# Pooled attention with a gated mixing layer on one core: attention's steps at other places in the emission order, the tail queries' last 128 scores beside the last maximum, and the weights' scratch tile in three padded blocks

## The chip, the core and the metric

The kernel runs on one core of one Trainium2 chip. The metric is device time in microseconds (us), the median of several executions; less is better. The engines are named as the profile names them: PE multiplies (PEld is its weight load), DVE is VectorE, ACT is ScalarE, POOL is GpSimd, SP issues the DMAs.

## The reference

All inputs are float32; q, k and v are 8 batches x 8 heads x 1152 x 64. What is computed, cut to its core:

```python
q_pool = q.reshape(B, H, S // 2, 2, D).mean(axis=3)          # 576 queries a head
scores = scale * np.matmul(q_pool, k.transpose(0, 1, 3, 2))  # 576 x 1152
scores = scores - np.max(scores, axis=-1, keepdims=True)
attn = np.exp(scores)
attn = attn / (np.sum(attn, axis=-1, keepdims=True) + 1e-09)
x = heads_side_by_side(np.matmul(attn, v))                   # 8 x 576 x 512
theta = x @ w_theta
y = w_tok_r @ (x * cos(theta)) + w_tok_i @ (x * sin(theta))  # over tokens
u = x + y
out = u + np.maximum(u @ w_ch, 0.0)
```

## The kernel before

The first part does attention, two heads at a time: 32 pairs `i`, in 18 score steps each (`u` is one of two halves of 288 pooled queries, `kt` one of nine blocks of 128 keys). The second part does the mixing layer; the change does not touch it.

For a pair, `prep_t` transposes keys and pooled queries on PE (`pt`, group 0 and group 1), ACT rounds them into `hi`, DVE takes the rest into `lo`. `maxpass` makes the row maxima: 12 steps of two matmuls (`pm`) and one DVE reduction each (L332). The last 64 queries of both heads share one tile, `tail`; `max_tail` multiplies it with keys 0 to 1023 (`px`) and, on L348, with the last 128 keys, whose result goes into the unused end of the next pair's `pt` tile; L351 and L352 reduce them. `max_nm` negates the maxima, `max_row` turns them (`pmt`) and copies them (`mT`), and `load_max` puts them as rows into `nmr` by four DMAs. `escore` is one score step: eight matmuls into one tile `pe` (hi x hi, hi x lo, lo x hi, and the maxima's row), then one exponential on ACT into `pc` (L393, 14 buffers). `av` is a run of matmuls of the nine `pc` of a half with `vn` (36 rows in the trace) into `pa`. `ssum` adds the `pc` up on POOL, `norm_sum` sums over the partitions (`pns`), and a chain of small DMAs with a reciprocal (L451) brings the divisors back for `norm_out` (L473).

All PSUM tiles of this part have two banks and go through four slots. `bank2` gives a new tile the slot that its own bookkeeping (the costs `HOLD`, three running clocks) holds to be free first. A tile's first matmul waits until the slot's last tile has been read.

The order on every engine is the order of emission. `plan` gives each step of each pair a position (18 positions to a pair, a score step at each whole one) and sorts them all. `burst` puts several steps at one position: with u = 0 it is transposes of group 1 for pair i+2, the maxima's row of pair i+1, `av` and the sums of pair i-1; with u = 1 it is `tail_prep` (transposes of group 0 for pair i+3 and `max_tail` of pair i+2) and `av`.

Beside all this, `weights` narrows the mixing layer's float64 weights to float32 in 18 jobs, one step at each position of `W_AT`. In `narrow` five DVE instructions with one input and one with two (L556) run on 128x512 or 128x576 words between the tiles `raw`, `wf` and `ws`.

Of the kernel before, what the change touches and what calls it, by code (L numbers as in the profile page):

```python
# [9 lines left out]
F32 = mybir.dt.float32  # L10
# [14 lines left out]
W_AT = (9.45, 9.5, 9.85, 10.5, 12.75, 18.0, 18.6, 19.25, 20.45)  # L25
# [4 lines left out]
MAX_AT1 = (-18.1, -16.8, -16.1, -15.35, -14.7, -14.0, -13.3, -12.6, -11.7, -10.3, -9.8, -9.0)  # L30
PLAN = {
    "load_q": -44.55,
    "load_k": -43.62,
    "pool_q": -35.35,
    "load_max": -7.6,
    "load_v": -7.0,
    "max_nm": -8.85,
    "norm_spread": 29.0,
    "norm_load": 29.15,
    "norm_recip": 37.5,  # L40
    "norm_save": 37.6,
    "norm_bcast": 37.7,
    "norm_out": 46.5,
    "norm_store": 46.6,
}
MAN = ("PE", "Activation", "DVE", "Pool", "SP")
BANKS = {}
SLOTS = 4
HOLD = {
    "e": (0.54, "a", 0.6),  # L50
    "pm": (0.17, "d", 0.95),
    "pt": (0.75, "ad", 2.1),
    "px": (0.6, "d", 1.55),
    "pa": (4.4, "a", 0.4),
    "mt": (0.2, "a", 0.3),
    "ns": (1.0, "a", 0.5),
    "pw": (0.75, "ad", 1.9),
}
BANKS2 = {"h": 1, "t": 1, "m": 4, "r": 2}
# [30 lines left out]
OT_LAG = 1.0  # L90
CH_BANK = "mrmr"
TINY = 2.0**-15
MAGIC = 12582912.0
# [8 lines left out]
def pooled_attention_moe_kernel(  # L102
# [58 lines left out]
    def bank2(kind, name):  # L161
        n = min(range(SLOTS), key=lambda k: slots[k])
        work, engines, after = HOLD[kind]
        clock["p"] = max(clock["p"], slots[n]) + work
# [43 lines left out]
    with ExitStack() as p1:  # L208
# [128 lines left out]
        def max_tail(i, pt):  # L337
# [7 lines left out]
            st["pm", 0] = pm  # L345
            if pt is None:
                pt = bank2("px", f"py{i}")
# [55 lines left out]

        def av(i, u):
            st = state[i]
            if u == 0:
                st["xu"] = nrm.tile([P, 2, HALF], F32, tag="xu", name=f"xu{i}", bufs=3)
            pa = bank2("pa", f"pa{i}_{u}")
            for kt in range(KT):
# [8 lines left out]
            nc.scalar.copy(st["xu"][:, u, :], pa[:, 0, 0:HALF])  # L418

        def norm_sum(i, px):  # L420
# [14 lines left out]
            sm = st["sm"] = sml.tile([P, HALF], F32, tag="sm", name=f"sm{i}", bufs=1)  # L435
            nc.scalar.activation(sm, px[:, 1, 0:HALF], AF.Identity, bias=eps)

        def norm_spread(i):
# [35 lines left out]

        def burst(i, u):
            if u == 0:
                if i + 2 < NPAIR:
                    prep_all(i + 2, 1)
                if i + 1 < NPAIR:
                    max_row(i + 1)  # L480
                av(i, u)
                if i > 0:
                    norm_sum(i - 1, bank2("ns", f"pns{i}"))
            else:
                tail_prep(i)
                av(i, u)

        def prep_all(i, g):
# [7 lines left out]

        def tail_prep(i):
            more = i + 3 < NPAIR
            if more:
                prep(i + 3)  # L500
                prep_t(i + 3, 0)
            if i + 2 < NPAIR:
                max_tail(i + 2, state[i + 3]["pt", 0] if more else None)
            if more:
                prep_hi(i + 3, 0)
                prep_lo(i + 3, 0)

# [8 lines left out]
        def weights():  # L516
# [7 lines left out]

            def fetch(parts, n):
                ws = wst.tile([P, SQ], F32, tag="ws", name="ws")
                raw = wst.tile(
                    [P, SQ, 2 if wide else 1], U32 if wide else F32, tag="raw", name="raw"
                )
                for dst, src in parts:  # L530
                    nc.sync.dma_start(raw[dst, 0:n], src)
                return raw, ws

            def narrow(raw, ws, R, n, g):
                dst = ws[0:R, 0:n].rearrange("a (t p) -> a p t", t=g)
                if not wide:
                    nc.vector.tensor_copy(
                        dst, raw[0:R, 0:n, 0].rearrange("a (p t) -> a p t", t=g)
                    )
# [7 lines left out]
                nc.scalar.activation(tl, lo, AF.Copy, scale=2.0**-44)  # L547
                nc.vector.tensor_scalar(f, hi, 0x7FFFFFFF, None, ALU.bitwise_and)
# [14 lines left out]
                yield  # L563
                nc.gpsimd.tensor_tensor(
                    dst,
                    f.bitcast(F32).rearrange("a (p t) -> a p t", t=g),
                    tl.rearrange("a (p t) -> a p t", t=g),
                    ALU.add,
                )
                yield  # L570
# [7 lines left out]
            def square(wv, c, dst):  # L578
                yield
                raw, ws = fetch([(slice(0, P), wv[:, c])], DM)  # L580
                yield
# [86 lines left out]
        def plan(i):  # L668
# [7 lines left out]
            if i < 2:  # L676
                at(PRO[i][1], 3, prep_all, i, 1)
                at(PRO[i][2], 3, max_tail, i, None)
            if i == 0:
                at(-7.8, 3, max_row, i)  # L680
            at(base + pl["load_max"], 7, load_max, i)
            at(base + pl["load_v"], 5, load_v, i)
# [8 lines left out]
            for u in range(2):  # L691
                at(base + AV_AT[u], 4, burst, i, u)
            for n, fn in (
# [10 lines left out]
        for i in range(NPAIR):  # L704
            plan(i)
        at(NU * NPAIR + 2, 9, lambda: norm_sum(NPAIR - 1, bank2("ns", "pend")))
        pw = ExitStack()
# [303 lines left out]
```

## Time and profile before

| | us |
|---|---|
| median of 3 runs (1397.08 to 1399.8) | 1399.42 |
| the profiled execution | 1395.23 |
| its span, first to last instruction | 1393.2 |
| first and last `pmt`, one in each of 32 pairs | 25.2 and 856.0 |

| engine | busy us | share of the span |
|---|---|---|
| PE | 1342.4 | 96% |
| POOL | 914.4 | 66% |
| DVE | 864.6 | 62% |
| ACT | 724.0 | 52% |

A busy PE is not a PE at its peak: a matmul that waits for its weights counts as busy. So for PE the starts of successive instructions say more than the busy share.

### The profile page before, as it was taken

The numbers are of one execution on the slowest core, as the hardware profiler recorded it, in microseconds if no ns is written. First come the engines' busy times: TensorE is split into PE (matmuls) and PEld (weight loads), VectorE is DVE, ScalarE is ACT, GpSimd is POOL, SyncE is SP. The second block draws the span as 40 slices with busy tenths as digits, with TensorE's granted clock in tenths as the row PEclk, the third lists the DMA queues.
The fourth block names the chain that finished last, engine by engine and source line by source line (L and its number), as shares of the span: only waits on it lengthen the run. The fifth ranks groups of instructions, "written<-read, shape, count | busy, mean of one in ns | idle before, by whom it ended". The sixth has DMA issues, their size and how long they took to land.

```text
span 1393.2 us, 29952 instructions
## 1 busy us (share of the span) xinstructions
PE 1342.4 (96%) x12178; PEld 1088.3 (78%) x12178; DVE 864.6 (62%) x1143; ACT 724.0 (52%) x1250; POOL 914.4 (66%) x672
## 2 busy tenths in 40 slices
PE   5999999999999999999999999899999999999998
PEld 3777777776777677777777777698999999999998
DVE  5867776776667776777677765465363453535442
ACT  1556565565556555565555565365454444445341
POOL 1789888989898998889898898742332322233220
PEclk9999999999999999999999999999999999999999
DMA  4334343334433444333443333221111211111111
GB/s 102 101 87 117 89 110 103 110 100 117 110 85 96 114 115 106 93 111 85 128 112 87 82 83 99 74 78 39 35 46 35 62 42 35 39 35 46 27 35 35
DMA packets 130906, 111.66 MB, mean 80 GB/s; under 512 B 95040, under 2 KB 95424, under 8 KB 130768
## 3 DMA queue, kind: packets, MB, share of 16 engines
q1 hardware_dynamic: 130592, 109.28, 28.9%
q8 instruction: 96, 1.57, 0.5%
q0 software_dynamic: 176, 0.46, 0.1%
q14 instruction: 42, 0.34, 0.1%
HBM read 88.29 MB, written 21.27 MB: 79 GB/s over the span
## 4 chain that ended last, share of the span: by engine, by line
PE 72%; DVE 15%; ACT 7%; DMA 3%; issue 2%; POOL 1%; SPq 0%; ACTq 0%; POOLq 0%; DVEq 0%
PE pe L390 18%; PE pa L411 17%; PE py L841 11%; PE pth L763 7%; PE pr L880 6%; DVE mx L332 5%; PE pt L285 4%; PE pm L325 3%; PE pns L427 2%; ACT pc L393 2%; PE pxn L751 1%; DVE r L785 1%; DVE r L786 1%; PE po L903 1%; DVE mx L351 1%
## 5 line engine op out<-in xcount | busy, mean ns | idle before, releaser
L402 POOL TENSOR_TENSOR ss<-ss,pc 128x576 f32<-128x576 f32 x384 | 561.8, 1463 | 68.9 <-ACT pc L393 45.8
L332 DVE TENSOR_REDUCE mx<-pm 128x2 f32<-128x768 f32 x384 | 347.5, 951 | 125.6 <-PE pm L325 124.0
L393 ACT ACTIVATE pc<-pe 128x576 f32<-128x576 f32 x576 | 364.8, 652 | 98.2 <-PE pe L390 85.6
L411 PE MATMUL pa<-pc,vn 128*64 128x288 f32 x2304 | 293.5, 409 | 0.9 <-PE pmt L362 0.8
L814 POOL TENSOR_TENSOR Z<-ab,Z 128x512 fp32r<-128x512 f32 x40 | 51.6, 1291 | 309.4 <-ACT Z L810 274.1
L411 PEld LDWEIGHTS pa<-pc,vn 128*64 128x64 f32 x2304 | 162.2, 137 | 109.4 <-issue 5.4
L841 PE MATMUL py<-wtk,Z 128*128 128x288 f32 x1728 | 242.0, 297 | 0.0
L841 PEld LDWEIGHTS py<-wtk,Z 128*128 128x128 f32 x1728 | 233.2, 189 | 1.5 <-ACT Z L810 0.2
L390 PE MATMUL pe<-hi 64*128 64x288 f32 x1152 | 202.7, 345 | 12.3 <-DVE mx L332 7.3
L390 PEld LDWEIGHTS pe<-hi 64*128 64x128 f32 x1152 | 109.5, 184 | 83.2 <-ACT pc L393 34.0
L390 PE MATMUL pe<-nmr,oner 64*128 64x288 f32 x1152 | 171.9, 291 | 2.2 <-DMA nmr<-mT 2.2
L390 PE MATMUL pe<-lo,hi 64*128 64x288 f32 x1152 | 172.2, 293 | 0.0
L390 PE MATMUL pe<-hi,lo 64*128 64x288 f32 x1152 | 172.0, 292 | 0.0
L325 PE MATMUL pm<-hi 64*128 64x384 f32 x768 | 137.5, 354 | 9.1 <-DVE mx L332 4.7
L390 PEld LDWEIGHTS pe<-nmr,oner 64*128 64x128 f32 x1152 | 110.5, 185 | 2.6 <-DMA nmr<-mT 2.6
L390 PEld LDWEIGHTS pe<-lo,hi 64*128 64x128 f32 x1152 | 111.0, 186 | 0.0
L390 PEld LDWEIGHTS pe<-hi,lo 64*128 64x128 f32 x1152 | 110.4, 185 | 0.0
L312 DVE TENSOR_TENSOR lo<-pt,hi 128x768 fp32r<-128x768 f32 x64 | 67.6, 1056 | 64.5 <-ACT hi L301 64.5
L880 PEld LDWEIGHTS pr<-us,wch 128*128 128x128 f32 x768 | 104.5, 188 | 2.0
L880 PE MATMUL pr<-us,wch 128*128 128x288 f32 x768 | 105.8, 295 | 0.0
L301 ACT CAST hi<-pt 128x768 fp32r<-128x768 f32 x64 | 56.2, 878 | 84.4 <-DVE mx L352 68.1
L402 POOL TENSOR_TENSOR ss<-pc,pc 128x576 f32<-128x576 f32 x64 | 93.8, 1466 | 5.9 <-ACT pc L393 5.9
(105 smaller groups left out, 1657.9 us busy)
## 6 DMA issues: line engine op xcount, KB each, us to landing
qn<-in_q_dram SPq DMA_DIRECT2D x32, 576.0 KB
kn<-in_k_dram SPq DMA_DIRECT2D x64, 288.0 KB
vn<-in_v_dram SPq DMA_DIRECT2D x32, 576.0 KB
dn<-ro SPq DMA_DIRECT2D x64, 144.0 KB
xd<-xu SPq DMA_DIRECT2D x32, 288.0 KB
xT<-xd SPq DMA_DIRECT2D x8, 1152.0 KB
out_dram<-on SPq DMA_DIRECT2D x23, 192.0 KB
out_dram<-on SPq DMA_DIRECT2D x23, 128.0 KB
```

What stands on the lines that cost most here:

```text
L285: nc.tensor.transpose(out=pt[:, n, c : c + R], in_=src.rearrange("p h d -> p (h d)"), identity=ident[0:R, 0:R],)
L301: nc.scalar.copy(hi, src)
L312: nc.vector.tensor_tensor(lo, src, hi.bitcast(F32), ALU.subtract)
L325: nc.tensor.matmul(pm[:, h, 0:W], hi[hs, Q0 + j * P : Q0 + (j + 1) * P], hi[hs, K0[3 * g] : K0[3 * g] + W], start=True, stop=True,)
L332: nc.vector.tensor_reduce(mx[:, j : j + 5 : 4, g : g + 1], pm[:, :, 0:W], AX.X, ALU.max)
L390: nc.tensor.matmul(pe[:, h, 0:HALF], w[hs], x[hs], start=(n == 0), stop=(n == 3))
L393: nc.scalar.activation(pcs[u, kt], pe[:, :, 0:HALF], AF.Exp, scale=SC)
L402: nc.gpsimd.tensor_tensor(st["ss", u], first, st["pc"][u, kt], ALU.add)
L411: nc.tensor.matmul(pa[hs, 0, 0:HALF], st["vn"][:, h, kt, :], st["pc"][u, kt][:, h, :], start=(kt == 0), stop=(kt == KT - 1),)
L763: nc.tensor.matmul(th, xs[c][:, j * P : (j + 1) * P], ws[:, c], start=(n == 0), stop=(n == 11))
L841: nc.tensor.matmul(st["py", c, u][:, 0:HALF], Z[zi][:, c * P : (c + 1) * P], wtk[wi][:, kw, u * HALF : (u + 1) * HALF], start=(i == 0 and ...
L880: nc.tensor.matmul(pr[u][:, 0:HALF], wch[wi][:, c, e * P : (e + 1) * P], st["us", ui][:, c, u * HALF : (u + 1) * HALF], start=(n == 0), st ...
```

## The change

- All steps get positions of their own in place of `burst` and `tail_prep`: the transposes, their `hi` and `lo`, the tail copy, `max_tail` and the maxima's row by the table `PREP_AT`, the sums by `NS_AT`. All other positions and the costs in `HOLD` have new numbers. `av` can now be split into pieces, but the table asks for nine steps in one piece.
- The tail's product with the last 128 keys goes into free columns of the last `pm` tile of `maxpass`, with its reduction right behind that tile's. The separate tile `py` that some pairs used is gone.
- In `narrow` the scratch tile `wf` has three blocks of a third of the columns, 194 words apart. The one-input instructions now have one side in three blocks and the other side plain; 512 columns become 513, with one more small DMA for the last one in 8 of the 18 jobs. The first shift writes `wf` instead of `raw`.

```diff
-MAX_AT = (-24.9, -23.65, -22.55, -20.85, -19.55, -18.8, -15.55, -14.35, -13.5, -11.6, -10.2, -9.15)
-SS_LAG = 4.5
-AV_AT = (10.35, 19.25)
+MAX_AT = (-25.08, -24.951, -24.126, -21.989, -17.714, -16.703, -16.481, -16.035, -13.864, -10.761, -9.027, -7.903)
+SS_LAG = 5.493
+AV_AT = (((10.593, 9),), ((19.957, 9),))
+PREP_AT = {'t0': -34.901, 'hi0': -34.757, 'px': -9.4, 'lo0': -34.733, 't1': -26.381, 'hi1': -26.225, 'lo1': -25.86, 'tail': -25.662, 'row': -7.096}
+NS_AT = 29.431
...
+WF_COLS = 194
...
+                    rest = j == 3 and g == 2
+                    if rest:
+                        nc.tensor.matmul(
+                            pm[:, 0, W:], st["tail"], hi[:, K0[8] : K0[8] + P], start=True, stop=True
+                        )
                     nc.vector.tensor_reduce(
                         mx[:, j : j + 5 : 4, g : g + 1], pm[:, :, 0:W], AX.X, ALU.max
                     )
+                    if rest:
+                        nc.vector.tensor_reduce(mx[:, 8, 2:3], pm[:, 0, W:], AX.X, ALU.max)
...
-            nc.tensor.matmul(
-                pt[:, 0, 3 * P :], tl, hi[:, K0[8] : K0[8] + P], start=True, stop=True
-            )
             nc.vector.tensor_reduce(mx[:, 8, 0:2], pm, AX.X, ALU.max)
-            nc.vector.tensor_reduce(mx[:, 8, 2:3], pt[:, 0, 3 * P :], AX.X, ALU.max)
...
-                lo, hi = raw[0:R, 0:n, 0], raw[0:R, 0:n, 1]
-                f = wst.tile([P, SQ], U32, tag="wf", name="wf")[0:R, 0:n]
+                n = 3 * -(-n // 3)
+                f = wst.tile([P, 3, WF_COLS], U32, tag="wf", name="wf")[0:R, :, 0 : n // 3]
...
+                lo, hi = three(raw[0:R, 0:n, 0]), three(raw[0:R, 0:n, 1])
                 tl = lo.bitcast(F32)
-                mk = ws[0:R, 0:n]
-                nc.vector.tensor_scalar(lo, lo, 8, None, ALU.logical_shift_right)
+                mk = three(ws[0:R, 0:n])
+                nc.vector.tensor_scalar(f, lo, 8, None, ALU.logical_shift_right)
```

Three places show what moves. The names carry no pair number: in what follows the `pe` rows are pair 14's, `pm` and `px` are pair 15's unless it says otherwise. First, PE just behind `av` of the half u = 1. Before:

```order
L390 MATMUL pe_02_5782<-hi_4941 128x288 x2
L390 MATMUL pe_02_5782<-lo_4942,hi_4941 128x288 x2
L390 MATMUL pe_02_5782<-hi_4941,lo_4942 128x288 x2
L390 MATMUL pe_02_5782<-nmr_108,oner 128x288 x2
L325 MATMUL pm_20_5792<-hi_5341 128x384 x2
L390 MATMUL pe_03_5800<-hi_4941 128x288 x2
L390 MATMUL pe_03_5800<-lo_4942,hi_4941 128x288 x2
L390 MATMUL pe_03_5800<-hi_4941,lo_4942 128x288 x2
L390 MATMUL pe_03_5800<-nmr_108,oner 128x288 x2
L325 MATMUL pm_21_5810<-hi_5341 128x384 x2
```

The same place after:

```order
L372 MATMUL pe_02_5781<-hi_4939 128x288 x2
L372 MATMUL pe_02_5781<-lo_4940,hi_4939 128x288 x2
L372 MATMUL pe_02_5781<-hi_4939,lo_4940 128x288 x2
L372 MATMUL pe_02_5781<-nmr_108,oner 128x288 x2
L372 MATMUL pe_03_5793<-hi_4939 128x288 x2
L372 MATMUL pe_03_5793<-lo_4940,hi_4939 128x288 x2
L372 MATMUL pe_03_5793<-hi_4939,lo_4940 128x288 x2
L372 MATMUL pe_03_5793<-nmr_108,oner 128x288 x2
L372 MATMUL pe_04_5807<-hi_4939 128x288 x2
L372 MATMUL pe_04_5807<-lo_4940,hi_4939 128x288 x2
L372 MATMUL pe_04_5807<-hi_4939,lo_4940 128x288 x2
L372 MATMUL pe_04_5807<-nmr_108,oner 128x288 x2
```

Before, score and maximum steps take turns; after, three score steps stand in a row and then one maximum step (`pm_22`) follows.

Second, PE around `av` of the half u = 0 (`pmt` is pair 15's row of maxima, `pt_16` pair 16's transposes of group 1). Before:

```order
L390 MATMUL pe_11_5911<-nmr_108,oner 128x288 x2
L285 MATMUL pt_16_5921<-ident,qp_5722 128x96 x6
L285 MATMUL pt_16_5921<-ident,kn_5573 128x128 x3
L362 MATMUL pmt_5935<-ident,nm_5901 9x128
L411 MATMUL pa_0_5940<-pc_00_5707,vn_5594 64x288 x2
```

After (here `pm_00` and `pm_01` are pair 16's and `pns` the sums of pair 13):

```order
L398 MATMUL pa_0_5939<-pc_08_5864,vn_5713 64x288 x2
L344 MATMUL pmt_5960<-ident,nm_5932 9x128
L307 MATMUL pm_00_5965<-hi_5731 128x384 x2
L372 MATMUL pe_12_5970<-hi_4939 128x288 x2
L372 MATMUL pe_12_5970<-lo_4940,hi_4939 128x288 x2
L372 MATMUL pe_12_5970<-hi_4939,lo_4940 128x288 x2
L372 MATMUL pe_12_5970<-nmr_108,oner 128x288 x2
L307 MATMUL pm_01_5980<-hi_5731 128x384 x2
L419 MATMUL pns_5984<-ss_13_5450,ones 32x288
```

The row of maxima moved from ahead of the nine `av` steps to right behind them; the sums, which stood directly behind `av`, now stand behind a score step and two maximum steps; the transposes of group 1 moved up by a score and a maximum step.

Third, DVE over the same time (`lo` is pair 16's). Before:

```order
L332 TENSOR_REDUCE mx_5598<-pm_30_5853 128x2
L332 TENSOR_REDUCE mx_5598<-pm_31_5870 128x2
L332 TENSOR_REDUCE mx_5598<-pm_32_5886 128x2
L357 TENSOR_REDUCE nm_5901<-mx_5598 128x9
L548 TENSOR_SCALAR wf<-raw 128x512
L550 TENSOR_SCALAR ws<-wf 128x512
L552 TENSOR_SCALAR wf<-ws 128x512
L312 TENSOR_TENSOR lo_5737<-pt_16_5921,hi_5736 128x960
```

After:

```order
L319 TENSOR_REDUCE mx_5565<-pm_30_5859 128x2
L334 TENSOR_REDUCE mx_5565<-px_5876 128x2
L319 TENSOR_REDUCE mx_5565<-pm_31_5881 128x2
L530 TENSOR_SCALAR wf<-raw 128x3x171
L532 TENSOR_SCALAR ws<-wf 128x513
L319 TENSOR_REDUCE mx_5565<-pm_32_5925 128x2
L323 TENSOR_REDUCE mx_5565<-pm_32_5925 128x1
L294 TENSOR_TENSOR lo_5732<-pt_16_5903,hi_5731 128x960
L339 TENSOR_REDUCE nm_5932<-mx_5565 128x9
```

The reduction of `px` moved here from the other half of the pair, and the negated maxima `nm` now stand behind two weight instructions and `lo`.

## Rows read from the trace of the kernel before

**Rows 1.** Busy time over pairs 1 to 29 of attention, by engine.

```profile
core 0: us, PE busy (x) PEld busy (x) DVE busy (x) ACT busy (x) POOL busy (x), PEclk, DMA share, GB/s
58.50:842.50 784.00, 766.14 (x8053) 565.50 (x8051) 569.46 (x672) 457.54 (x798) 698.98 (x507) 1.00 0.38 101
```

**Rows 2.** Tile `pmt`, once a pair: ns min/median/max, first and last start.

```profile
L362 PE MATMUL pmt<-ident,nm x32: 269/273/372, 25.2 to 856.0; 128*9 128x128 f32 x32
```

**Rows 3.** Timeline of PE, 400 to 430 us: start, us, engine, line, idle before.

```profile
401.40 0.69 PE L427 MATMUL pns<-ss,ones 128*32 128x288 f32 x8
...
402.51 0.40 PE L390 MATMUL pe<-hi 64*128 64x288 f32 x2
...
410.59 0.29 PE L390 MATMUL pe<-nmr,oner 64*128 64x288 f32 x2
410.81 0.87 PE L285 MATMUL pt<-ident,kn 128*128 128x128 f32 x6
...
412.14 4.59 PE L411 MATMUL pa<-pc,vn 128*64 128x288 f32 x36
416.65 0.40 PE L390 MATMUL pe<-hi 64*128 64x288 f32 x2
...
417.29 0.34 PE L325 MATMUL pm<-hi 64*128 64x384 f32 x2
417.46 0.29 PE L390 MATMUL pe<-hi 64*128 64x288 f32 x2
...
417.99 0.34 PE L325 MATMUL pm<-hi 64*128 64x384 f32 x2
418.20 0.40 PE L390 MATMUL pe<-hi 64*128 64x288 f32 x2
...
424.52 0.71 PE L285 MATMUL pt<-ident,qp 96*128 96x96 f32 x6
...
425.61 4.59 PE L411 MATMUL pa<-pc,vn 128*64 128x288 f32 x36
```

**Rows 4.** Timeline of the other engines, and PE, in the same stretch.

```profile
417.49 1.35 ACT L393 ACTIVATE pc<-pe 128x576 f32<-128x576 f32 x2 [0.32 <-PE pe L390]
...
418.54 1.45 DVE L545 TENSOR_SCALAR raw<-raw 128x512 uint32<-128x512 uint32 x1
...
420.91 0.40 PE L390 MATMUL pe<-hi 64*128 64x288 f32 x2 [1.22 <-DVE mx L332]
```

**Rows 5.** Groups by shape: busy us, mean ns, idle us before, releasers.

```profile
L332 DVE TENSOR_REDUCE mx<-pm 128x2 f32<-128x768 f32 x384 | 347.5, 951 | 125.6 <-PE pm L325 124.0
L390 PE MATMUL pe<-hi 64*128 64x288 f32 x1152 | 202.7, 345 | 12.3 <-DVE mx L332 7.3 <-DVE wtk L184 0.8 <-ACT tail L308 0.8
L390 PE MATMUL pe<-lo,hi 64*128 64x288 f32 x1152 | 172.2, 293 | 0.0
L351 DVE TENSOR_REDUCE mx<-px 128x2 f32<-128x1024 f32 x32 | 39.0, 1219 | 18.9 <-PE px L342 18.7
L312 DVE TENSOR_TENSOR lo<-pt,hi 128x960 fp32r<-128x960 f32 x32 | 37.0, 1155 | 32.2 <-ACT hi L301 32.2
L451 DVE RECIPROCAL rc<-rc 128x9 f32<-128x9 f32 x32 | 6.5, 204 | 1.2 <-DMA rc<-rd 1.2
L610 PE MATMUL pwt<-ident,ws 128*128 128x128 f32 x32 | 5.2, 286 | 0.0
```

**Rows 6.** Who waited for whom, PE's weight loads: us, times, longest.

```profile
PEld pe L390 <- ACT pc L393: 34.0, 134, 0.7
PEld pe L390 <- issue: 23.2, 55, 0.5
```

**Rows 7.** Single lines: ns min/median/max, first and last start.

```profile
L552 DVE TENSOR_SCALAR wf<-ws x18: 444/1375/2096, 61.0 to 839.7; 128x512 uint32<-128x512 uint32 x8, 128x576 uint32<-128x576 uint32 x8, 64x576 uint32<-64x576 uint32 x2
L556 DVE SCALAR_TENSOR_TENSOR wf<-raw,wf x18: 677/1480/2393, 66.1 to 843.8; 128x512 uint32<-128x512 uint32 x8, 128x576 uint32<-128x576 uint32 x8, 64x576 uint32<-64x576 uint32 x2
L370 SPq DMA_DIRECT2D nmr<-mT x64: 612/636/1033, 30.5 to 858.0; - x64
```

More of the change, by code (lines that the diff above doesn't have):

```diff
@@ L163, in bank2 @@
         work, engines, after = HOLD[kind]
+        psum["slot"] = n
         clock["p"] = max(clock["p"], slots[n]) + work
@@ L402, in ssum, with av @@
             nc.gpsimd.tensor_tensor(st["ss", u], first, st["pc"][u, kt], ALU.add)
-        def av(i, u):
+        def av(i, u, first, n):
             st = state[i]
[L406 to L409, printed above, removed]
+            if first == 0:
+                if u == 0:
+                    st["xu"] = nrm.tile([P, 2, HALF], F32, tag="xu", name=f"xu{i}", bufs=3)
+                st["pa", u] = bank2("pa", f"pa{i}_{u}")
+                st["slot"] = psum["slot"]
+                if n < KT:
+                    slots[st["slot"]] = 1e9
+            pa = st["pa", u]
+            for kt in range(first, first + n):
                 for h, hs in enumerate(HEADS):
@@ L417, in av @@
                     )
-            nc.scalar.copy(st["xu"][:, u, :], pa[:, 0, 0:HALF])
+            if first > 0:
+                clock["p"] += AV_WORK * n
+            if first > 0 and first + n == KT:
+                slots[st["slot"]] = clock["p"] + 0.8
+            if first + n == KT:
+                nc.scalar.copy(st["xu"][:, u, :], pa[:, 0, 0:HALF])
         def norm_sum(i, px):
@@ L436, in norm_sum, with norm_sums @@
             nc.scalar.activation(sm, px[:, 1, 0:HALF], AF.Identity, bias=eps)
+        def norm_sums(i):
+            norm_sum(i, bank2("ns", f"pns{i}"))
         def norm_spread(i):
@@ L495, in prep_all, with prep_first @@
                 prep_tail(i)
[L497 to L506, printed above, removed]
+        def prep_first(i):
+            prep(i)
+            prep_t(i, 0)
         def norm_store(i):
@@ L523, in words, with fetch @@
                 return w.bitcast(U32).rearrange("r (e o) -> r e o", o=2)
-            def fetch(parts, n):
+            def fetch(parts, n, more=None):
                 ws = wst.tile([P, SQ], F32, tag="ws", name="ws")
@@ L531, in fetch, with three @@
                     nc.sync.dma_start(raw[dst, 0:n], src)
+                if wide and more is not None:
+                    nc.sync.dma_start(raw[:, n : n + 1], more)
                 return raw, ws
             def narrow(raw, ws, R, n, g):
-                dst = ws[0:R, 0:n].rearrange("a (t p) -> a p t", t=g)
                 if not wide:
                     nc.vector.tensor_copy(
-                        dst, raw[0:R, 0:n, 0].rearrange("a (p t) -> a p t", t=g)
+                        ws[0:R, 0:n].rearrange("a (t p) -> a p t", t=g),
+                        raw[0:R, 0:n, 0].rearrange("a (p t) -> a p t", t=g),
                     )
                     return
-                lo, hi = raw[0:R, 0:n, 0], raw[0:R, 0:n, 1]
-                f = wst.tile([P, SQ], U32, tag="wf", name="wf")[0:R, 0:n]
+                n = 3 * -(-n // 3)
+                f = wst.tile([P, 3, WF_COLS], U32, tag="wf", name="wf")[0:R, :, 0 : n // 3]
+                def three(x):
+                    return x.rearrange("a (b c) -> a b c", b=3)
+                lo, hi = three(raw[0:R, 0:n, 0]), three(raw[0:R, 0:n, 1])
                 tl = lo.bitcast(F32)
-                mk = ws[0:R, 0:n]
-                nc.vector.tensor_scalar(lo, lo, 8, None, ALU.logical_shift_right)
+                mk = three(ws[0:R, 0:n])
+                nc.vector.tensor_scalar(f, lo, 8, None, ALU.logical_shift_right)
                 yield
-                nc.scalar.activation(tl, lo, AF.Copy, scale=2.0**-44)
+                nc.scalar.activation(tl, f, AF.Copy, scale=2.0**-44)
                 nc.vector.tensor_scalar(f, hi, 0x7FFFFFFF, None, ALU.bitwise_and)
@@ L563, in narrow @@
                 yield
[L564 to L569, printed above, removed]
+                if g == 1:
+                    dst, a, b = mk, f.bitcast(F32), tl
+                else:
+                    dst = ws[0:R, 0:n].rearrange("a (t b r) -> a b r t", t=g, b=3)
+                    a = f.bitcast(F32).rearrange("a b (r t) -> a b r t", t=g)
+                    b = tl.rearrange("a b (r t) -> a b r t", t=g)
+                nc.gpsimd.tensor_tensor(dst, a, b, ALU.add)
                 yield
@@ L677, in plan @@
                 at(PRO[i][1], 3, prep_all, i, 1)
-                at(PRO[i][2], 3, max_tail, i, None)
+                at(PRO[i][2], 3, max_tail, i)
             if i == 0:
                 at(-7.8, 3, max_row, i)
+            for n, (name, fn, args) in enumerate((
+                ("t0", prep_first, (i,)), ("hi0", prep_hi, (i, 0)), ("lo0", prep_lo, (i, 0)),
+                ("t1", prep_t, (i, 1)), ("hi1", prep_hi, (i, 1)), ("lo1", prep_lo, (i, 1)),
+                ("tail", prep_tail, (i,)), ("px", max_tail, (i,)), ("row", max_row, (i,)),
+            )):
+                if i >= (3, 3, 3, 2, 2, 2, 2, 2, 1)[n]:
+                    at(base + PREP_AT[name], 3, fn, *args)
             at(base + pl["load_max"], 7, load_max, i)
@@ L691, in plan @@
             for u in range(2):
-                at(base + AV_AT[u], 4, burst, i, u)
+                first = 0
+                for pos, n in AV_AT[u]:
+                    at(base + pos, 4, av, i, u, first, n)
+                    first += n
+            at(base + NS_AT if i < NPAIR - 1 else NU * NPAIR + 2, 9, norm_sums, i)
             for n, fn in (
```

52 lines of the change are left out of this document (7 added, 45 removed).

## Prediction

> **What bounds the kernel now.** I read the busy time of the attention stage first. Over 784 us of it PE is busy for 766.14 at a granted clock of 1.00; POOL comes next with 698.98, then DVE with 569.46 [rows 1]. So PE sets the pace, and POOL leaves room to shorten a pair only from 26.8 to about 23.9 us. The maxima's row is transposed once in each of 32 pairs, from 25.2 to 856.0 us [rows 2]: (856.0 - 25.2) / 31 = 26.80 us a pair.
>
> Then I read PE's timeline for what a pair would take if nothing waited [rows 3]. A score step is 0.53 (417.46 to 417.99), a maximum step 0.17 (417.29 to 417.46), a run of `av` 4.51 (412.14 to 416.65), transposes of group 0 with the tail's products 1.33 (410.81 to 412.14), group 1 with the maxima's row 1.09 (424.52 to 425.61), the sums 1.11 (401.40 to 402.51). That makes 18 x 0.53 + 12 x 0.17 + 2 x 4.51 + 1.33 + 1.09 + 1.11 = 24.13. Two more things belong to it. The last two matmuls before a transposition take 0.22 in place of 0.13 (410.59 to 410.81), twice a pair; the first score step behind `av` or the sums takes 0.64 (416.65 to 417.29), 0.11 more than the others, again twice. So 24.53, and 0.17 for the weights' transposes (5.2 us over 31 pairs [rows 5]): 24.70. The other 2.10 us of a pair are waits.
>
> These waits have two sources. The first is slot reuse. The score step at 416.65 ends at 417.29; its exponential starts at 417.49 and takes 0.68 (1.35 for two), so its slot is free at 418.17 [rows 3, 4]. Only 0.87 us of PE work (a maximum, a score, a maximum) lies between, and the step at 418.20 that takes the slot shows 0.40 in place of 0.29: its weights could not be loaded ahead. Over the run the first matmuls of score steps take 345 ns against 293 for the others [rows 5], and PE's loads waited 134 times for an exponential, 34.0 us in all [rows 6]. The second is DVE: a weight instruction of 1.45 us at 418.54 puts the maxima behind it, and PE stands 1.22 us at 420.91 [rows 4].
>
> **The change part by part.** *Slots and turn-taking.* With the new numbers the slots rotate over three other tiles, in most places 1.22 us of PE work (two scores and a maximum). The exponential needs 0.20 + 0.68 = 0.88, so 0.34 is to spare. What eats it is ACT itself: three scores in a row take PE 1.59, their exponentials 2.04, so each adds 0.15 of backlog. Walking through the new order with these durations, I find one late slot between `av` of u = 1 and `av` of u = 0, and two in the other half: 3 x 0.11 = 0.33 us a pair. Maximum steps, which took turns with scores (one in 0.70 us of PE, 0.95 of DVE [rows 5]), are now spread over the pair, so I charge no more for them. What is late next is ACT, by about 0.1 us at several places.
>
> *Weight instructions.* The five with one input took 444 ns at best and 1375 in the median for L552; that spread shows a wait for something outside DVE, and POOL is busy nine tenths of that time [rows 1, 7]. In three blocks I take 0.68, the best of L556 with two inputs, which gets no faster form [rows 7]. The bounds are 0.44 and the old 1.38. That takes 5 x 0.7 = 3.5 us off DVE in each of 18 jobs. In the trace such a delay reached PE when maxima stood right behind it. I leave 0.07 us a pair for it, so waits after are 0.40 in all, with bounds of 0.2 and 1.0.
>
> [...]
>
> *Changes of shape on PE.* This is what the change adds. Score and maximum steps use 64 rows of the array, all else 128. Where the shape changes, the next weights are not loaded ahead: 0.09 at the end of the old shape, and 0.11 more where the new one is a score (above). Before, a pair has seven changes, two of them into 64 rows. In the new order `px`, both transposes, the maxima's row, the sums and the 128 last tail scores stand apart, each between 64-row steps: fourteen changes, six into 64 rows. So four more at 0.20 into 64 rows, four more out of them at 0.14 (0.09 is shown; the entry I take as half of 0.11), and one fewer between wide shapes: 0.80 + 0.56 - 0.14 = 1.22. Bounds: eight at 0.09 is 0.72, eight at 0.20 is 1.60. That a change counts each time is shown by the 55 loads of score steps that waited on "issue" alone, 23.2 us [rows 6], about two a pair.
>
> *What costs nothing.* The products of the tail stay the same in number. Without the 128 scores in `pt`, `hi` of group 0 need not wait for them; `av` covered that. The reciprocal comes less far behind the sums, some 9.7 us by my walk in place of 12; it waited 1.2 us in the whole run [rows 5], and an `av` run of 4.5 us stands behind it as cover. Two queues are moved past each other: on SP the maxima's four DMAs (0.64 each [rows 7]) now start only after `av`, end 2.9 us behind it and have 6.3 us of PE work until their first reader; the new q load stands between the two small loads of the divisors. On POOL the pooling of queries moves into the pause behind the first half's sums. Eight small DMAs are added on an SP that has time. Pair 0, the last pair and the mixing layer stay.
>
> *The sum.* 24.70 + 1.22 + 0.40 = 26.32 us a pair against 26.80: 0.48 less, over about 30 pairs 14.4, rounded with the bounds this wide to 15. The profiled execution of 1395.23 (span 1393.2, 2 us around it) would come to 1380. The median of the runs lies 4.2 higher at 1399.42, so I predict 1384.
>
> **The rivals.** *Shape changes are free.* If PE loaded weights ahead across them, the 1.22 falls away: 30 x (26.80 - 25.10) = 51, so 1348. Against it stand the 0.40 rows behind `av` and the sums, 416.65 and 402.51 [rows 3]. [...]
>
> *PE waits behind `av` for the maxima* (slower). The maxima's row now stands directly behind the run, and DVE must first do, from `px` on, 1.22 + 0.95 + two weight instructions + 0.95 + 1.16 [rows 5] and two small ones. That is 5.6 with weight instructions of 0.68, 7.0 with the old 1.38, plus the small ones; PE takes some 7.4 over the same part. It decides the sign where DVE arrives about a us late in nearly every pair: then 26.32 + 1.0 = 27.32, 30 x 0.52 = 16 slower, 1415. For it speaks that all 18 score steps behind stand in PE's queue; against it that DVE was busy only 73% of the stage [rows 1] and that most pairs have fewer than two weight instructions there.
>
> *The weights do not get quicker* (the blocks do not do what they could). One delay of 1.22 on PE is shown [rows 4]; one such in most of 18 jobs gives back about 15, so 1399, the same. The spread in [rows 7] speaks against it only if its cause goes away.
>
> *ACT becomes the bound.* If the three-in-a-row scores cost the full 1.0 of my bound in waits, 26.92: 30 x 0.12 = 4 slower, 1403.
>
> **How the numbers follow.** I give my forecast (1364 to 1396) 0.58, free changes 0.10, weights no quicker 0.12, ACT as the bound 0.08, PE behind `av` 0.12. The lower end of the forecast's case is changes at 0.72 with waits of 0.2: 25.62, 35 less, 1364. For 8 in 10 I leave out most of the free changes below and the wait behind `av` above: 1360 to 1403. A measurement of this kernel can tell about 0.2% (2.8 us) from no change. Faster takes the forecast and the free changes and a little of the third, 0.69; the same 0.13; slower 0.18.
>
> **What would show each step.** In the changed profile the mean of the first score matmuls should fall from 345 towards 310 ns, and PE's loads that wait for exponentials from 134 to some tens; the loads waiting on "issue" should rise, on maxima too, by some seven a pair. L552's successor should have a narrow spread about 0.7. Two rows of `pmt` should lie 26.3 apart on average. PE idle in front of `pmt` by DVE would show the slower rival. I am wrong if the pair shortens without fewer late slots, or if changes of shape show no price.

## The result and the profile after

The changed kernel takes 1379.78 us in the median (1378.34 to 1381.76, four runs), the kernel before on the same chip 1398.53: a ratio of 0.9881, with a 95% interval of 0.9869 to 0.9894. The forecast was 1384. Its profiled execution took 1378.9 us, with a span of 1377.1; 16.1 less than the span before.

First the rows that answer to [rows 1, 2]: busy time over pairs 1 to 29 (PE, PEld, DVE, ACT, POOL, clock, DMA share, GB/s), then `pmt`, once over all pairs and once over three of them, and the runs of `av`, before (L411) and after (L398).

```profile
58.50:842.50 784.00, 777.78 (x8227) 576.19 (x8223) 556.01 (x686) 441.18 (x811) 708.13 (x515) 1.00 0.39 102
...
L344 PE MATMUL pmt<-ident,nm x32: 277/278/373, 25.3 to 842.7; 128*9 128x128 f32 x32
...
L344 PE MATMUL pmt<-ident,nm x3: 277/278/278, 288.1 to 339.8; 128*9 128x128 f32 x3
...
L411 PE MATMUL pa<-pc,vn x2304: 406/406/457, 48.5 to 890.8; 128*64 128x288 f32 x192
...
L398 PE MATMUL pa<-pc,vn x2304: 406/406/457, 48.1 to 873.0; 128*64 128x288 f32 x192
```

By `pmt`, a pair now takes (842.7 - 25.3) / 31 = 26.37 us in place of 26.80. But the change moved this marker: from pair 1 on it stands behind a run of `av` in place of ahead of it, and the whole run falls into the first distance, which went from 23.09 to 27.38. The runs of `av` stayed nearly where they were, so they compare like with like: from the first to the last it is 842.3 us before and 824.9 after. That is 17.4 less, or 0.56 a pair where `pmt` shows 0.43. The first `av` comes 0.4 sooner, and what follows the last one takes 1.7 longer (502.4 before, 504.1 after); together these are the 16.1 of the span.

The two pairs from 288.1 to 339.8 took 25.85 each, and 13 of the 31 distances between starts of `pmt` lie between 25.84 and 25.88. Before, these distances spread evenly, from 26.03 up to 28.74 once the first and the last are left out. So the pairs without disturbance have become alike, and what is left sits in the others.

PE's timeline over a pair, as in [rows 3] (start, us, engine, line, tile):

```profile
403.24 4.59 PE L398 MATMUL pa<-pc,vn 128*64 128x288 f32 x36
407.75 0.45 PE L307 MATMUL pm<-hi 64*128 64x384 f32 x2
408.04 0.30 PE L372 MATMUL pe<-hi 64*128 64x288 f32 x2
...
408.56 0.29 PE L372 MATMUL pe<-hi 64*128 64x288 f32 x2
...
409.09 0.29 PE L372 MATMUL pe<-hi 64*128 64x288 f32 x2
...
409.62 0.34 PE L307 MATMUL pm<-hi 64*128 64x384 f32 x2
...
411.54 0.30 PE L372 MATMUL pe<-hi 64*128 64x288 f32 x2
...
412.17 0.74 PE L331 MATMUL px<-hi,tail 128*128 128x512 f32 x3
412.83 0.44 PE L307 MATMUL pm<-hi 64*128 64x384 f32 x2
413.11 0.29 PE L372 MATMUL pe<-hi 64*128 64x288 f32 x2
```

Behind `av` three scores stand in a row, 0.53 apart: no slot is late. The price of the places shows at `px`: the score ahead of it ends 0.63 behind its start (411.54 to 412.17), 0.10 more than 0.53, and the maximum step behind it takes 0.28 (412.83 to 413.11) where it takes 0.17 elsewhere. So a change of shape costs 0.10 at the end of the 64-row step and 0.11 at the start of the next one.

The groups that answer to [rows 5], then the waits that answer to [rows 6] (us, times, longest):

```profile
L372 PE MATMUL pe<-hi 64*128 64x288 f32 x1152 | 177.9, 301 | 0.7 <-DVE wtk L166 0.3 <-DVE mx L319 0.2
L307 PE MATMUL pm<-hi 64*128 64x384 f32 x768 | 146.6, 389 | 5.7 <-DVE mx L319 2.3 <-ACT hi L283 2.1 <-DVE wtk L166 0.5
...
PEld pe L372 <- ACT pc L375: 2.7, 10, 0.5
PEld pe L372 <- issue: 6.5, 35, 0.4
PEld pm L307 <- issue: 28.3, 80, 0.5
PEld pm L307 <- DVE mx L319: 6.7, 11, 1.3
PEld pmt L344 <- issue: 16.4, 31, 3.3
PEld pm L316 <- issue: 6.7, 32, 0.3
PEld px L331 <- issue: 5.1, 31, 0.3
```

The first matmuls of score steps fell from 345 ns to 301, nearly the 293 of the others. Loads waited for an exponential 10 times instead of 134. The entries into 64 rows now fall on maximum steps (80 waits on "issue") rather than on scores.

Two weight instructions, as in [rows 7] (ns min/median/max): L552 has become L534, L556 has become L538.

```profile
L534 DVE TENSOR_SCALAR wf<-ws x18: 676/734/754, 59.9 to 824.2; 128x513 uint32<-128x513 uint32 x8, 128x576 uint32<-128x576 uint32 x8, 64x576 uint32<-64x576 uint32 x2
L538 DVE SCALAR_TENSOR_TENSOR wf<-raw,wf x18: 682/1146/1889, 60.7 to 826.5; 128x513 uint32<-128x513 uint32 x8, 128x576 uint32<-128x576 uint32 x8, 64x576 uint32<-64x576 uint32 x2
```

With one input the best case got slower (444 to 676) and the rest much quicker (median 1375 to 734, maximum 2096 to 754). With two inputs the spread stayed.

### The profile page after: what moved, and what is told of

Same layout as the page of the kernel before. It is cut to its first block, busy times and chain, and to the rows that moved or that the text cites. A ratio compares the mean times of both kernels' runs of the same rounds, so it can differ in the third digit from the quotient of the medians.

```text
span 1377.1 us, 29856 instructions
## 1 busy us (share of the span) xinstructions
PE 1336.4 (97%) x12178; PEld 1087.0 (79%) x12178; DVE 840.2 (61%) x1143; ACT 699.2 (51%) x1250; POOL 910.8 (66%) x672
## 4 chain that ended last, share of the span: by engine, by line
PE 82%; DVE 6%; ACT 5%; POOL 4%; issue 1%; DMA 1%; SPq 0%; POOLq 0%; ACTq 0%; DVEq 0%
PE pe L372 21%; PE pa L398 19%; PE py L834 11%; PE pth L756 7%; PE pm L307 7%; PE pr L873 6%; PE pt L267 4%; POOL ss L384 3%; PE pns L419 2%; PE px L331 1%; DVE mx L319 1%; PE pxn L744 1%; DVE r L778 1%; DVE r L779 1%; PE po L896 1%
## 5 line engine op out<-in xcount | busy, mean ns | idle before, releaser
L319 DVE TENSOR_REDUCE mx<-pm 128x2 f32<-128x768 f32 x384 | 360.9, 951 | 184.2 <-PE pm L307 167.1
L375 ACT ACTIVATE pc<-pe 128x576 f32<-128x576 f32 x576 | 343.7, 654 | 82.6 <-PE pe L372 77.4
L398 PE MATMUL pa<-pc,vn 128*64 128x288 f32 x2304 | 293.5, 409 | 4.3 <-ACT tail L290 2.2
L398 PEld LDWEIGHTS pa<-pc,vn 128*64 128x64 f32 x2304 | 159.7, 137 | 115.8 <-issue 5.9
L372 PE MATMUL pe<-hi 64*128 64x288 f32 x1152 | 177.9, 301 | 0.7 <-DVE wtk L166 0.3
L307 PE MATMUL pm<-hi 64*128 64x384 f32 x768 | 146.6, 389 | 5.7 <-DVE mx L319 2.3
L410 ACT COPY xu<-pa 128x288 f32<-128x288 f32 x64 | 25.6, 399 | 178.8 <-PE pa L398 178.8
L307 PEld LDWEIGHTS pm<-hi 64*128 64x128 f32 x768 | 72.6, 188 | 51.3 <-issue 28.3
```

What stands on the lines that cost most here:

```text
L307: nc.tensor.matmul(pm[:, h, 0:W], hi[hs, Q0 + j * P : Q0 + (j + 1) * P], hi[hs, K0[3 * g] : K0[3 * g] + W], start=True, stop=True,)
L319: nc.vector.tensor_reduce(mx[:, j : j + 5 : 4, g : g + 1], pm[:, :, 0:W], AX.X, ALU.max)
L372: nc.tensor.matmul(pe[:, h, 0:HALF], w[hs], x[hs], start=(n == 0), stop=(n == 3))
L375: nc.scalar.activation(pcs[u, kt], pe[:, :, 0:HALF], AF.Exp, scale=SC)
L398: nc.tensor.matmul(pa[hs, 0, 0:HALF], st["vn"][:, h, kt, :], st["pc"][u, kt][:, h, :], start=(kt == 0), stop=(kt == KT - 1),)
```

## The experiments

The theory, as the prediction has it: a pair is its dense work, plus a price for each change of shape, plus waits where a slot or a maximum is late. Rivals are named with each run. Unless said otherwise the ratio is to the kernel before on the same chip, three rounds.

**Old turn-taking in the new order.** Only the places of the maximum steps go back:

```diff
-MAX_AT = (-25.08, -24.951, -24.126, -21.989, -17.714, -16.703, -16.481, -16.035, -13.864, -10.761, -9.027, -7.903)
+MAX_AT = (-24.9, -23.65, -22.55, -20.85, -19.55, -18.8, -15.55, -14.35, -13.5, -11.6, -10.2, -9.15)
```

> The changed kernel with the old places of the twelve maximum steps, which take turns with the score steps again; all else, the fourteen changes of shape a pair too, stays. Theory (late slots are what the change removes): most score steps find their slot after 0.87 us of PE work again, so the first score matmuls go back from 301 ns towards 330, waits return by 0.8 us a pair, 25 us: about 1405, slower than before. Rival (the blocks or the other moves made the gain): within 4 us of 1380.

1407.16 us, 1.0077 (1.0062 to 1.0092): 27 us lost against the changed kernel. The waits of PE's loads, and the score group:

```profile
PEld pe L372 <- ACT pc L375: 27.7, 92, 0.8
PEld pe L372 <- issue: 19.8, 66, 0.4
PEld pe L372 <- DVE mx L319: 8.1, 37, 0.8
...
L372 PE MATMUL pe<-hi 64*128 64x288 f32 x1152 | 209.5, 358 | 2.9 <-DVE mx L319 1.5 <-ACT pc L375 0.9
```

The late slots are back, and the changes of shape have not gone. That is what the sum says: the waits return, the price stays, and the kernel is slower than before.

**New turn-taking in the old order.** The reverse, from the kernel before; the last three places stay, since the row of maxima stands ahead of `av` there:

```diff
-MAX_AT = (-24.9, -23.65, -22.55, -20.85, -19.55, -18.8, -15.55, -14.35, -13.5, -11.6, -10.2, -9.15)
+MAX_AT = (-25.08, -24.951, -24.126, -21.989, -17.714, -16.703, -16.481, -16.035, -13.864, -11.6, -10.2, -9.15)
```

> The kernel before with the changed kernel's places for the first nine of the twelve maximum steps and nothing else; transposes, the tail's product, the row of maxima and the sums stay in their bursts beside av (7 shape changes a pair, not 14). Theory (the steps that the change sets apart are what keeps a slot's next user far off; without them in between, maxima and scores that stand in a row get slots back after 0.53 to 0.87 us of PE work, and three reductions of 0.95 us stand right behind av): PE waits for DVE mx and the gain is gone or more: 1400 to 1425 us. Rival (the gain is in the turn-taking and the seven more shape changes are a mere price, 1.22 us a pair): PE is saved 30 x (1.22 + 0.4) or so, 1340 to 1365.

1398.33 us, 1.0013 (1.0000 to 1.0026). No gain, if a little less loss than expected; the rival's 1340 to 1365 is out. The waits for exponentials do fall, from 34.0 us [rows 6] to 15.1, but those for maxima rise, from 10.1 to 39.3 (the profile is of the slowest of ten executions, 1402.87, so part of the 39.3 is its own):

```profile
PEld pe L390 <- DVE mx L332: 10.1, 13, 1.4
...
PEld pe L390 <- DVE mx L332: 39.3, 72, 3.5
PEld pe L390 <- ACT pc L393: 15.1, 62, 0.5
```

The first line is the kernel before, the other two this run.

So neither half of the new order gains alone. The places of the maxima and the places of the rest have to fit.

**A turn-taking that fits the old order.** From the kernel before, one maximum step behind mostly every second score; nothing is set apart, so the seven changes of shape stay seven:

```diff
-MAX_AT = (-24.9, -23.65, -22.55, -20.85, -19.55, -18.8, -15.55, -14.35, -13.5, -11.6, -10.2, -9.15)
+MAX_AT = (-25.0, -23.9, -21.9, -19.9, -18.9, -16.9, -15.9, -13.9, -12.9, -11.9, -10.9, -9.15)
```

> The kernel before with one maximum step behind every second score step, inside the old bursts: 7 slots of a pair come back after 0.7 or 0.87 us in place of 11, no shape change is added. Theory (0.11 us for each late slot): 0.4 us a pair less, 30 pairs, 12 us: 1382 to 1390. Rival (what the kernel before loses in its waits for DVE stays or grows): 1393 to 1400.

1383.21 us, 0.9897 (0.9878 to 0.9917), as the theory says. From its profile:

```profile
PEld pe L390 <- ACT pc L393: 11.9, 52, 0.7
PEld pm L325 <- ACT pc L393: 5.8, 27, 0.2
...
L390 PE MATMUL pe<-hi 64*128 64x288 f32 x1152 | 201.4, 343 | 4.0 <-DVE wtk L184 0.8 <-DVE rc L451 0.7 <-ACT pc L393 0.6
...
L362 PE MATMUL pmt<-ident,nm x32: 272/272/372, 25.0 to 842.1; 128*9 128x128 f32 x32
```

The waits of scores for exponentials fell from 134 to 52 (27 more are now at maximum steps), and PE's idle time ahead of scores from 12.3 us [rows 5] to 4.0. `pmt` did not move here, and a pair takes (842.1 - 25.0) / 31 = 26.36, 0.44 less than before; the changed kernel gains 0.56 by `av`. One line reaches most of the gain: what the change sets apart was a way to it, not a condition. The mean of the first score matmuls hardly moved, 343 ns: here the entries into 64 rows fall on scores, as before, and about a hundred loads of scores still wait some 0.1 us for an exponential, which the list of waits, from 0.15 us up, leaves out. That number alone would have hidden the gain.

**The three blocks alone, and left out.** The blocks in the kernel before, and the changed kernel without them:

```diff
-                f = wst.tile([P, SQ], U32, tag="wf", name="wf")[0:R, 0:n]
+                n = 3 * -(-n // 3)
+                f = wst.tile([P, 3, WF_COLS], U32, tag="wf", name="wf")[0:R, :, 0 : n // 3]
...
```

> The kernel before with the three padded blocks alone. Theory: the five instructions with one input fall from 1.2 to 1.4 us to 0.68 to 0.75, DVE loses 33 us of busy time, but only the few waits in which PE stood behind such an instruction go: 5 to 15 us faster, 1384 to 1394. Rival (the blocks are the whole gain): 1380. Rival (DVE has room, so nothing): 1398.

> The changed kernel with the old scratch tile, the order unchanged. Theory: in the new order maxima have more room, so longer weight instructions cost PE less than before: 3 to 12 us slower than the changed kernel, 1383 to 1392; the median of the one-input instructions back over 1 us. Rival (the blocks are the whole gain): 1398.

Alone, 1393.45 us, 0.9981 (0.9971 to 0.9990): 2.9 us on that chip, less than the 5 to 15 expected, though the time lies in the range. Left out, 1383.81, 0.9907 (0.9890 to 0.9923): 4 more than the changed kernel's 1379.78, from another chip; the two intervals just overlap. Without the blocks the loads of maximum steps wait twice as long as the 6.7 us shown above. The first line is that wait, the second the successor of L552 in this run:

```profile
PEld pm L307 <- DVE mx L319: 14.4, 18, 2.7
...
L527 DVE TENSOR_SCALAR wf<-ws x18: 420/820/1547, 59.8 to 830.8; 128x512 uint32<-128x512 uint32 x8, 128x576 uint32<-128x576 uint32 x8, 64x576 uint32<-64x576 uint32 x2
```

Its median was expected over 1 us and is 0.82. Summed over the run, the five one-input instructions take DVE 97.1 us in the kernel before and 64.7 with the blocks alone, 32 less, as expected; in the changed order they take 69.2 without the blocks and 64.4 with them. So the blocks quicken these instructions as the prediction says, but the new order by itself had already taken most of that time away. They are worth 3 to 4 us, where the third rival put 15 on them, and what they still spare in the new order is mainly the longest ones (up to 1.67 us against 0.75).

**Blocks on top of the fitted turn-taking** (five rounds; both edits above in the kernel before):

> The kernel before with one maximum step behind every second score step inside the old bursts (7 shape changes a pair) and with the scratch tile in three padded blocks; no step is set apart. Theory (the gains of turn-taking, 14 us, and of the blocks, 3 to 4 us, come from different waits and add up): 1379 to 1382, as fast as the changed kernel or within 0.2% of it, so that what the change sets apart was not needed for its gain. Rival (both take the same waits of PE for maxima behind weight instructions): 1383 or more.

1384.89 us, 0.9914 (0.9899 to 0.9929), no better than 0.9897 without the blocks. The rival is nearer: in this order the blocks add nothing that can be measured. The changed kernel has the lowest ratio of all, 0.9881, but its interval overlaps that of the fitted turn-taking (0.9878 to 0.9917).

**The tail's last 128 scores alone**, in the kernel before:

```diff
+                    if rest:
+                        nc.tensor.matmul(
+                            pm[:, 0, W:], st["tail"], hi[:, K0[8] : K0[8] + P], start=True, stop=True
+                        )
...
-            nc.vector.tensor_reduce(mx[:, 8, 2:3], pt[:, 0, 3 * P :], AX.X, ALU.max)
```

> The kernel before with only the tail queries' last 128 scores moved beside the last maximum step (and its reduction behind that step's), all positions as before. Theory (the products stay the same in number): one shape change between a maximum step and the 128 scores is added, 0.09 to 0.2 us a pair, one wait of hi for pt falls away that av covered anyway, and the reduction of 0.1 to 0.2 us now stands just ahead of the negated maxima, where av does not cover it: 1396 to 1403. Rival (hi of group 0 comes earlier and lo with it, which frees DVE for the maxima): 1385 to 1393.

1395.99 us, 0.9990 (0.9980 to 0.9999): nothing worth the name, as expected (1396 to 1403, with before at 1397.12).

**One place taken back: the sums.** In the changed kernel the sums go directly behind the maxima's row, which saves one change of shape:

```diff
-NS_AT = 29.431
+NS_AT = 28.91
```

> The changed kernel with the sums directly behind the maxima's row, so that av, row and sums stand together: one change of shape into 64 rows fewer a pair. Theory (each change costs about 0.2 us): 0.2 us a pair or 6 us faster, 1374, less up to 3 us for two slots a pair that now return after 0.87 us. Rival (changes of shape are hidden in the new order): 1380 or, by the slots, slower.

1385.84 us, 0.9926 (0.9912 to 0.9941): 6 slower, where 1374 was expected. `pmt` in two undisturbed pairs, and the wait:

```profile
L344 PE MATMUL pmt<-ident,nm x3: 277/278/278, 289.6 to 341.8; 128*9 128x128 f32 x3
...
PEld pe L372 <- DVE mx L319: 14.5, 29, 0.6
```

The two pairs took 26.11 each against 25.85. In each pair one score now waits for a maximum, since without the sums between them its slot comes back after 0.87 us of PE work. The 1.1 us of sums were cover for DVE. The price of a change was saved and a wait of twice its size bought.

**The sums again, with the maxima spread**, and its control without the sums' move:

```diff
-MAX_AT = (-25.08, -24.951, -24.126, -21.989, -17.714, ...
+MAX_AT = (-25.08, -23.95, -21.95, -19.95, -17.714, ...
```

> The changed kernel, with the sums directly behind the maxima's row (one pair of shape changes fewer, 13 in place of 14) and the 2nd to 4th maximum step moved so that no slot comes back after less than 1.2 us of PE work. Theory (a pair is its dense time plus its late slots): the 0.17 us a pair that joining the sums gave in the dense part stay, and the wait of 0.34 us for maxima that ate them is gone: about 25.70 us in a quiet pair against 25.86, 1374 to 1377 us. Rival (the sums serve as cover for DVE wherever the maxima stand): the wait for maxima is there again, 1384 or more, and PE's loads of score steps wait some 10 us or more for maxima in all.

> The changed kernel with the 2nd to 4th maximum step moved as in the kernel before this one, the sums where the change puts them (14 shape changes). It is the control. Theory: the number of shape changes is the same and no slot was late there, so the time is that of the changed kernel, 1378 to 1383. Rival (spreading the maxima is itself worth something, or does harm): outside 1375 to 1386.

1386.56 us (0.9933, 0.9918 to 0.9948) and 1385.80 (0.9928, 0.9913 to 0.9942). Both miss. Against the control, the joined sums cost nothing any more (the intervals lie on each other), and the wait for maxima fell from 14.5 us to 8.0; but the 4 to 6 us that joining should have given did not come either. The control itself lost 6 us. Its own score group and the wait for maxima:

```profile
L372 PE MATMUL pe<-hi 64*128 64x288 f32 x1152 | 184.9, 315 | 3.7 <-DVE mx L319 1.9 <-DVE wtk L166 1.3
...
PEld pe L372 <- DVE mx L319: 5.1, 11, 1.5
...
294.01 0.96 DVE L319 TENSOR_REDUCE mx<-pm 128x2 f32<-128x768 f32 x1 [0.67 <-PE pm L307]
...
295.03 0.19 PEld L372 LDWEIGHTS pe<-hi 64*128 64x128 f32 x2
```

In eleven pairs a score now waits for a maximum, nine times about 0.3 us. And by the starts on PE the score step number 7 of the half comes late in 28 pairs, mostly by 0.1, though its slot returns after the same 1.22 us that suffice in the changed kernel. The last two rows show why. The maximum step whose slot it takes gives way on PE at 293.81; its reduction starts 0.20 later and ends at 294.97, and only then can the weights of the score be loaded. So a maximum holds its slot for 1.16 us, where a score holds it for 0.88. Loads that stand about 0.1 us until a reduction ends are under the 0.15 us from which waits are listed; in the trace there are 47 here and one in the changed kernel. Walked through with the planner's own rule, from pair 2 on no score step of the changed kernel takes a maximum's slot after less than 1.56 us of PE work; here over 70 do so after 1.23 to 1.35. A distance of 1.2 us for every slot, by which these places were chosen, is thus enough behind a score and too short behind a maximum.

**One place taken back: the tail's product**, directly behind the transposes of group 0:

```diff
-PREP_AT = {'t0': -34.901, 'hi0': -34.757, 'px': -9.4, ...
+PREP_AT = {'t0': -34.901, 'hi0': -34.757, 'px': -16.9, ...
```

> The changed kernel with the tail queries' product px directly behind the transposes of group 0: 12 shape changes a pair in place of 14, but score steps then come closer together and 25 more of all slots come back after 0.87 us. Theory: the two changes fewer are worth 0.20 + 0.14 by the prediction's prices, some 0.2 to 0.34 us a pair, 6 to 10 us in all: 1370 to 1375 if DVE takes px without delaying a maximum. The same theory says that a wait of DVE's 1.2 us reduction of px in front of a maximum step would eat that; then 1380 to 1388 and PE's loads wait for DVE mx. Rival (shape changes cost little): 1378 to 1382 with no wait for maxima.

1439.20 us, 1.0309 (1.0293 to 1.0324): far outside what either side expected. The timeline around one `av`, and the wait over the run:

```profile
398.89 1.22 DVE L334 TENSOR_REDUCE mx<-px 128x2 f32<-128x1024 f32 x1 [0.17 <-PE px L331]
400.04 0.95 DVE L294 TENSOR_TENSOR lo<-pt,hi 128x768 fp32r<-128x768 f32 x1
...
401.13 4.59 PE L398 MATMUL pa<-pc,vn 128*64 128x288 f32 x36 [1.72 <-DVE lo L294]
...
PE pa L398 <- DVE lo L294: 46.4, 26, 2.3
```

The reduction of `px` now stands on DVE ahead of `lo`, and the next `av` gets the slot of the transposes that `lo` still reads. PE stands 1.7 us ahead of `av` in most pairs. Moving one step also moved the slots that the planner gives to the steps behind it; the expectation looked at scores and maxima and left out `av`.

**The row of maxima back ahead of `av`**, which measures the cover that the slower rival doubted:

```diff
-'row': -7.096}
+'row': -7.45}
```

> The changed kernel with the transposition of the maxima's row ahead of the nine av steps of u = 0 in place of behind them. It measures the cover that the prediction's slower rival doubted. Theory (av covers DVE's chain from the last maxima over two weight instructions and lo to the negated maxima): without it PE stands about 1.5 to 3 us in front of the row in each pair, by DVE, part of which the shape change saved (0.2) gives back: 1420 to 1460. Rival (DVE is through before av begins): no wait, one shape change fewer, 1374 to 1380.

1501.16 us, 1.0749 (1.0731 to 1.0767). The wait is where the theory has it, and the loss larger than it says. The wait over the run, one place of PE's timeline, and the same place by stretches (columns as in [rows 1]):

```profile
PE pmt L344 <- DVE nm L339: 79.6, 31, 3.9
...
417.69 0.28 PE L344 MATMUL pmt<-ident,nm 128*9 128x128 f32 x1 [2.40 <-DVE nm L339]
418.06 6.28 PE L398 MATMUL pa<-pc,vn 128*64 128x288 f32 x36
...
407.00:415.00 8.00, 8.00 (x97) 7.01 (x95) 4.97 (x5) 6.05 (x10) 5.77 (x5) 1.00 0.40 103
418.06:421.20 3.14, 3.14 (x14) 1.66 (x16) 2.27 (x2) 0.23 (x1) 3.14 (x3) 0.53 0.07 13
421.20:424.20 3.00, 3.00 (x24) 1.53 (x20) 0.00 (x0) 0.00 (x0) 0.39 (x1) 0.92 0.00 0
```

PE waits 79.6 / 31 = 2.57 us in each pair. Behind a wait of 2.40 us `av` takes 6.28 us, not 4.59, under a granted clock of 0.53 in its first half and 0.92 in the second. Over the run the 31 runs of `av` behind the row are 1.43 us longer in the mean than the 4.51 of the others. 2.57 + 1.43 less 0.2 for the saved change of shape is 3.8; from the first to the last `av` a pair became 4.0 longer. And it gives the margin of the changed kernel: 4.51 us of `av` hide a wait of 2.57, so DVE is some 1.9 us early. The changed kernel's own trace agrees: there `nm` ends 2.10 us ahead of `pmt` in the median, and 0.6 in the closest pair behind the first.

## Why the prediction came out

- **The period.** Predicted 26.32 us, 0.48 less than before. Measured by `pmt` it is 26.37, which looks closer than it is, since the marker moved; by `av` a pair became 0.56 shorter. The 26.80 averages in a first and a last distance of 23.09 and 24.91; the 29 between them went from 26.99 to 26.41. The pairs gained 17.4 us in place of 14.4, and the end, which the prediction left as it was, lost 1.7. The two partly cancel, so that the profiled time (1378.9 against 1380) agrees this well is in part luck. The 4.2 us from there to the median were noise: the changed kernel's median is only 0.9 above. The mechanism that carries it, late slots that go away, is shown from both sides: they come back with the old turn-taking (27 us), and most go in the old order too with another one (14 us).
- **Changes of shape.** Out of 64 rows and back was priced at 0.14 + 0.20 = 0.34. At `px` the rows show 0.10 ahead of it and 0.11 behind it, and `px` itself takes 0.66 (412.17 to 412.83) in place of the 0.55 before (411.44 to 411.99): 0.32. An undisturbed pair of 25.85 is 1.32 longer than the 24.53 of dense work, where 1.22 was priced. (The prediction counts the queries' transposes as 128 rows; [rows 3] show 96.) The rival of free changes (1348) is out. That weights are not loaded ahead across them shows in the changed kernel's trace: at all 336 changes between 64 and 128 rows in pairs 1 to 29 a load starts at most 3 ns ahead of its matmul, and between two matmuls with 64 rows 130 ns ahead in the median. 31 of the 32 `px`, with 128 rows behind scores with 64, have a load that waited on "issue". What else the price is made of was not tested by itself.
- **Waits, right in sum and wrong in parts.** The prediction put 0.33 us a pair on three late slots and 0.07 on the weights. The 10 waits that are left make 2.7 us in the run, 0.09 a pair. The weights are what is left. The nine pairs that hold their transposes take 27.0 to 28.7 us, 27.41 in the mean, and took 27.42 before: they gained nothing. The 20 others, without the first and the last distance, went from 26.80 to 25.96. Above 25.85 the nine cost 14.1 us, 0.45 a pair over the run, of which 0.17 were booked as transposes. In the longest PE does them in 0.7 and then stands 2.20 ahead of `av`, whose slot waits for `lo` and the tail's copy:

```profile
572.91 0.62 PE L593 MATMUL pwt<-ident,ws 128*128 128x128 f32 x4
...
574.18 1.15 DVE L294 TENSOR_TENSOR lo<-pt,hi 128x960 fp32r<-128x960 f32 x1
575.36 0.42 ACT L290 CAST tail<-pt 64x64 fp32r<-64x64 f32 x2 [1.91 <-DVE lo L294]
...
575.84 1.43 PE L398 MATMUL pa<-pc,vn 128*64 128x288 f32 x10 [2.20 <-ACT tail L290]
```

- **Weight instructions.** 0.68 was predicted, 0.73 measured, with the narrow spread that was named. The 0.68 was borrowed from L556, on the view that two inputs allow nothing faster; in the kernel before its 18 took 677 ns or more, and the 72 of L804 in the mixing layer, also with two inputs and 128x512, 681 or more. With three blocks on one side the best case of one input slows from 444 to 676; why it comes to the pace of two inputs no run shows. Time was won all the same, since the old median was 1375. But the order has its share in that fall: without the blocks it brings the median to 820.
- **PE behind `av`** (slower). Its condition was asked the right way: the margin was worked out as 7.4 - 5.6 = 1.8 less two small instructions, and the run with the row ahead of `av` gives 1.9. Its price was too small: in that run a wait of 2.57 us came with another 1.43 in `av`, where the granted clock was down to 0.53 at the place shown.
- **Weights no quicker.** The third rival put 15 us on them from one delay of 1.22; they are worth 3 to 4. One row was taken for the typical one, and the new order's own effect on these instructions was not foreseen.
- **"Issue" waits.** Seven more a pair were expected; the rows show about five (330 against 177 in the run). A load that waits for something else as well may be booked under that.
- **What costs nothing** held for the waits: PE waited for no divisor and once for rows of maxima. It did not hold for the end, which is 1.7 us longer.

Open: why the blocks are worth about 4 us in the changed order, where they take 4.8 us off DVE, and nothing in the fitted old one, where they take 28 off it (92.7 to 64.6); no run tells the two orders' DVE queues apart. Why the end became longer is open too.

## What to carry to other kernels

Where an engine seems full, first look at how far apart in its own work the users of a buffer stand, and compare it with the time that this buffer's own reader needs (0.88 us behind a score, 1.16 behind a maximum); moving the steps between them can pay without taking any work out, and a single table of places may do most of what a whole new order does. Check too that the mark by which a period is measured stands at the same place before and after. A step that stands between two users is cover, also when its place costs something: joining it elsewhere can cost more than it saves, and a planner may then hand the late buffer to a step nobody looked at. And an order is one thing: its places for the maxima, taken over alone, were worth nothing here.

## What the runs showed of the hardware

- With the row ahead of `av`, a wait of 2.40 us in front of PE was followed by a granted clock of 0.53 for 3.1 us and 0.92 for the next 3.0, and cost 1.7 us beyond itself. 25 of the 31 runs of `av` behind such waits were longer than the usual 4.51; the other six, behind waits of 1.6 to 2.8 us, were not.
- DVE's one-input instructions lost their best time with three blocks on one side (444 ns to 676 at L552, L534 in the changed kernel) and were the quicker for it in sum: with only the blocks added to the kernel before, the five of all 18 jobs, 90 in number, take 64.7 us in place of 97.1. The long ones had POOL at work beside them. In the kernel before, the 16 of these 90 beside which POOL ran nothing took 414 to 472 ns; the other 74 took 444 to 2190, with a median of 1222. In the changed order without the blocks 74 again have POOL beside them, with a median of 720, so with POOL beside them they are not always long. With the blocks all lie between 673 and 767, with POOL at work or without. With two inputs L538 still took up to 1889.
